# Gram products of the first three batches written to the other half's lanes, copied back by ScalarE; mask of small weights on VectorE

## The chip, the cores and the metric

One core of one Trainium2 chip. The metric is the device time of one execution in microseconds; the time before is the median of three runs, 574.6 us (570.17 to 577.01). A measurement here separates differences of about 1%.

## The reference

A linear attention with the delta rule over 4 batches, 8 heads, 768 steps and a head dimension of 48, followed by a SoLU feed-forward layer with a norm:

```python
k_n = k / (norm(k) + 1e-6)
for t in range(768):
    y[t] = q[t] @ state
    state += beta[t] * outer(k_n[t], v[t] - state.T @ k_n[t])
x = y of all heads side by side              # 3072 x 384
h = x @ w_in                                 # 384 x 1024
solu = h * softmax(h)
ln = (solu - mean) / sqrt(var + 1e-6) * g_ln
out = ln @ w_out                             # 1024 x 384
```

Inputs arrive as float64 for the weights (read as pairs of 32-bit words) and the output is float32.

## The kernel before

**Chunks and units.** The 768 steps are cut into 12 chunks (`ch`) of 64. The four batches of the input are taken in pairs (`bp`), so that a tile has 128 lanes: 64 steps of one batch of the pair (`b2` = 0) and 64 of the other (`b2` = 1). A *unit* is one chunk of one pair with its 8 heads; there are 24.

**Gram.** For each unit TensorE forms, per head and half, the products k k^T (tile `gps_`, named gram in the profile) and k q^T (tile `pps`, named qk) from the loaded tile `kq`; both are float32, and each such product is two passes in the instruction stream. Gram and qk each take one of the two buffers of the PSUM ring `fl` (`ps_f`), which the later triangular-inverse steps (sps, mps) share. VectorE multiplies qk by the causal mask into `pm`; ScalarE copies gram out.

**Batches.** The 64-step triangular systems are inverted in 7 batches `m` of chunks: batch 0 holds chunk 0 (two units), batches 1 to 5 two chunks (four units) each, batch 6 chunk 11 (two units). Within a batch the inverse of the 32 x 32 blocks (`inv_begin`, 30 `inv_step`s, `inv_end`) is an elementwise recursion with the heads on the lanes. The lanes change by a transpose. The first three batches (`SPLIT = 3`, called *near*) do this on the chip: VectorE transposes `gct` (profile name gc) into `ginv`, and the recursion is split between VectorE and POOL in blocks of 16. From batch 3 on (*far*) ScalarE copies gram to `g`, a DMA takes it through DRAM (`gd`), and POOL alone runs the recursion (tiles y and itmp). `small_level` and `block_level` (tiles sps, ssb, mps, msb, zt) then assemble the 64 x 64 inverse on TensorE.

**Where gram lies.** In a far unit gram of half `b2` is written to the lanes of the other half, `gps_[half(1 - b2)]`, while qk goes to its own half. In a near unit only three 32 x 32 blocks of gram are formed, and each is written to its own lanes, in the first 32 columns or, for the off-diagonal block, the upper 32. So one copy over 128 lanes gives `gct` (the diagonal blocks) and two copies over 32 lanes give `gxt[m][0]` (profile name gx, the off-diagonal blocks).

**Chain and feed-forward.** `chain` runs the state recursion over units (kps, ups, cps, yps on TensorE; r, st on VectorE; u on ScalarE). `moe_h` forms h from a two-part float16 split of x and of w_in in 18 matmuls, and the softmax and statistics (e, pr, ph, pl, st). `moe_out` forms the output in 24 matmuls (ops, oc).

**Weights.** `to_f32` turns the float64 words of w_in (six pieces of 512 columns) and w_out (eight of 384) into float32 on the chip: ScalarE squares the upper word (`wc`), POOL turns that into a mask that is zero for very small weights and otherwise the scale, VectorE shifts and joins the words (`wf`, for w_out `wg`), and POOL multiplies by the mask. ScalarE then rounds to float16 (`win_hi`, `wout_hi`), and POOL (for w_in) or VectorE (for w_out) forms the remainder.

**Order.** Nothing is issued in the order of the program text. A recorder collects all operations with estimated costs (`ns=...`, or a base plus a price per element for each engine) and a priority that the streams set by due times. A list scheduler over the five queues (TensorE, VectorE, ScalarE, POOL and SP for the DMAs), which also counts the free buffers of each ring, writes the final order. A change in an estimate can therefore change the order of other work. On the chip each engine runs its list in order. All recorded operations show line 266 in the profile.

The lines of the code that the change and the steps of the prediction touch:

Of the kernel before, what the change touches and what calls it, by code (L numbers as in the profile page):

```python
# [11 lines left out]
ALU = mybir.AluOpType  # L12
# [5 lines left out]
C = 64  # L18
# [288 lines left out]
def kernel(  # L307
# [26 lines left out]
    pe = Engine(rec, "PE", nc.tensor, 0, 0, 200)  # L334
    dve = Engine(rec, "DVE", nc.vector, 150, 1.04, 80)
    act = Engine(rec, "ACT", nc.scalar, 110, 0.96, 100)
    gps = Engine(rec, "POOL", nc.gpsimd, 200, 1.8, 100)
# [3 lines left out]
    def half(b2):  # L341
        return slice(C * b2, C * b2 + C)

    def dims(b2):
        return slice(C * b2, C * b2 + D)
# [4 lines left out]
    for b2 in range(2):  # L350
        nc.gpsimd.affine_select(
            out=mask[half(b2)], in_=mask[half(b2)],
# [25 lines left out]
    def to_f32(u, raw, scale, n, nm):  # L378
        if raw.dtype == F32:
            dve.tensor_scalar(out=u, in0=raw[:, :n], scalar1=scale, scalar2=None, op0=ALU.mult)  # L380
            return
        w = raw.bitcast(I32)
        lo, hi = w[:, 0 : 2 * n : 2], w[:, 1 : 2 * n : 2]
        c = p2.tile([P, 512], F32, tag="wc", name=f"wc_{nm}")[:, :n]
        act.activation(c, hi.bitcast(F32), AF.Square)
        gps.tensor_scalar(out=c, in0=c, scalar1=(1.125 * 2.0**-15) ** 2, scalar2=scale, op0=ALU.is_ge, op1=ALU.mult)
        f = u
        u = u.bitcast(I32)
        dve.tensor_scalar(out=u, in0=hi, scalar1=3, scalar2=0x3FFFFFF8, op0=ALU.logical_shift_left, op1=ALU.bitwise_and)
        dve.scalar_tensor_tensor(out=u, in0=lo, scalar=29, in1=u, op0=ALU.logical_shift_right, op1=ALU.bitwise_or)  # L390
        dve.scalar_tensor_tensor(out=u, in0=hi, scalar=-(1 << 30), in1=u, op0=ALU.bitwise_and, op1=ALU.bitwise_or)
        gps.tensor_tensor(out=f, in0=f, in1=c, op=ALU.mult)

    def load_w_in(k, q, t0, t1):
        yield t0
        f = slice(512 * q, 512 * q + 512)
        raw = p3.tile([P, 512], w_in.dtype, tag="pr", name=f"wi_{k}_{q}")
        sp.dma_start(kb=512, out=raw, in_=w_in[k, q])
        yield t1
        w = p2.tile([P, 512], F32, tag="wf", name=f"wf_{k}_{q}")  # L400
        to_f32(w, raw, SC, 512, f"i{k}{q}")
        act.copy(out=win_hi[:, k, f], in_=w)
        gps.tensor_tensor(out=win_lo[:, k, f], in0=w, in1=win_hi[:, k, f], op=ALU.subtract)
# [7 lines left out]
    def load_w_out(k, t0, t1):  # L411
        yield t0
        raw = p10.tile([P, 512], w_out.dtype, tag="kq", name=f"wo_{k}")
        sp.dma_start(kb=384, out=raw[:, :DM], in_=w_out[k])
        raws.append(rec.ops[-1])
        yield t1
        w = p2.tile([P, 512], F32, tag="wf", name=f"wg_{k}")[:, :DM]
        to_f32(w, raw, g_sb[:, k : k + 1], DM, f"o{k}")
        act.copy(out=wout_hi[:, k], in_=w)
        dve.tensor_tensor(out=wout_lo[:, k], in0=w, in1=wout_hi[:, k], op=ALU.subtract)  # L420
# [17 lines left out]
    def units(m):  # L438
        return [(ch, bp) for ch in chunks_of(m) for bp in range(2)]
# [60 lines left out]
    gct, gxt = {}, {}  # L500

    def gram(m, u, t0):
        yield t0
        ch, bp = units(m)[u]
        k = kqt[ch, bp]
        near = m < SPLIT
        if near and u == 0:
            gct[m] = p2.tile([P, 32, 32], F32, tag="y", name=f"gc_{m}")
            if len(units(m)) == 2:
                gps.memset(gct[m][:, 2 * H :], 0.0)  # L510
            gxt[m] = p2.tile([P, 4 * H, 32], F32, tag="gx", name=f"gx_{m}"), None
        g = None if near else p2.tile([P, H, C], F32, tag="g", name=f"g_{ch}_{bp}")
        pm = p10.tile([P, H, C], F32, tag="pm", name=f"pm_{ch}_{bp}")
        pt[ch, bp] = pm
        gps_ = ps_f.tile([P, H, C], F32, tag="fl", name=f"gram_{ch}_{bp}")
        pps = ps_f.tile([P, H, C], F32, tag="fl", name=f"qk_{ch}_{bp}")
        lo, up = slice(0, 32), slice(32, 64)
        for h2 in range(0, H, 2):
            with rec.atomic():
                for h, b2 in hb[2 * h2 : 2 * h2 + 4]:  # L520
                    kk = k[dims(b2), h, 0]
                    if near:
                        for r, a, b, o in ((0, lo, lo, lo), (32, up, up, lo), (32, up, lo, up)):
                            pe.matmul(
                                ns=25, out=gps_[C * b2 + r : C * b2 + r + 32, h, o], lhsT=kk[:, a], rhs=kk[:, b],
                                start=True, stop=True,
                            )
                    else:
                        pe.matmul(ns=60, out=gps_[half(1 - b2), h], lhsT=kk, rhs=kk, start=True, stop=True)
                    pe.matmul(ns=60, out=pps[half(b2), h], lhsT=kk, rhs=k[dims(b2), h, 1], start=True, stop=True)  # L530
            rec.hold(pm)
        if near:
            hs = slice(H * u, H * u + H)
            act.copy(out=gct[m][:, hs], in_=gps_[:, :, lo])
            for r in (32, 96):
                act.copy(out=gxt[m][0][r : r + 32, hs], in_=gps_[r : r + 32, :, up])
        else:
            act.copy(out=g, in_=gps_)
        dve.tensor_tensor(out=pm, in0=pps, in1=mask.unsqueeze(1).to_broadcast([P, H, C]), op=ALU.mult)
        if near:  # L540
            return
        if u == 0:
            gdt[m] = dr.tile([P, 4, H, C], F32, tag="gd", name=f"gd_{m}")
        sp.dma_start(kb=256, out=gdt[m][:, u], in_=g)
        moved[m] = rec.ops[-1]
# [346 lines left out]
    for bp in range(2):  # L892
        add(once(-14 + .1 * bp, lambda bp=bp: load_kq(0, bp), lambda bp=bp: squares(bp)))
        add(gram(0, bp, -13.5 + .01 * bp))
        add(once(-13.25, lambda bp=bp: load_kv(0, bp), lambda bp=bp: fill_v(0, bp)))
        add(tlevel(0, bp, -12.9 + 0.1 * bp, -12.85 + 0.1 * bp), -2)
# [12 lines left out]
    for m in range(1, NB):  # L909
        f = 4 * m - 2  # L910
        nu = len(units(m))
        e = f if m > 1 else f - 2.5
        for u in range(nu):
            tg = e - 9 + 0.9 * u if m > 1 else -13.34 + 0.01 * u
            ch, bp = units(m)[u]
            add(once(tg - 0.9 if m > 1 else -13.36, lambda ch=ch, bp=bp: load_kq(ch, bp)))
            add(gram(m, u, tg))
            t = e - 1.9 + 0.9 * u
            add(tlevel(m, u, t, t + 0.4))
            add(once(f + u - 1.6 if m > 1 else -12.4 + 0.1 * u, lambda ch=ch, bp=bp: load_kv(ch, bp)))  # L920
            add(once(f + u - 0.9, lambda m=m, u=u: fill_v(m, u)))
        tn = e - 5.4 if m > 1 else -12.99
        add(begin(m, tn, tn + (0.5 if m > 1 else 0.01)))
        add(inversion(m, tn + 0.6 if m > 1 else -12.97, e - 2.6 if m > 1 else -12.5))
# [81 lines left out]
```

## Time and profile before

| | |
|---|---|
| median of three runs | 574.6 us (570.17 to 577.01) |
| profiled execution | 572.56 us, of which the span of the profile is 569.9 us |
| busy share of the span | TensorE 87%, VectorE 56%, POOL 46%, ScalarE 36% |
| instructions | 21929 |
| bytes moved by DMA | 62.34 MB |

Lines of the profile give a start and a length in microseconds, the engine (PE is TensorE's matmuls, PEld its weight loads, DVE VectorE, ACT ScalarE, POOL GpSimd, SPq the queue of DMA issues), the operation as output<-inputs by the names above, the shape, and in brackets how long the engine was idle before and what ended that. Rows of groups give the count, the busy time in us, the mean of one in ns, and the idle time before. Rows of windows give for each stretch its length and, in order, the busy time of PE, PEld, DVE, ACT and POOL with counts, then the granted clock of TensorE, the DMA share and GB/s. Matmuls are pipelined, so the busy time of a group of them is the time in which at least one ran.

### The profile page before, as it was taken

How to read it: one execution, taken by the hardware profiler on the slowest of the kernel's cores; microseconds unless marked ns; L12 is line 12 of the kernel's file. 1: busy time of each engine (PE TensorE's matmuls, PEld its weight loads, DVE VectorE, ACT ScalarE, POOL GpSimd, SP SyncE). 2: the span in 40 equal slices, each digit the busy share in tenths (PEclk: the TensorE clock that was granted, in tenths of full speed). 3: DMA queues.
4: the chain of work that ended last, by engine and by line, in shares of the span. 5: the costliest groups of instructions: out<-in, count | busy, mean ns of one | idle time of the engine just before them, and what ended most of it. 6: DMA issues, size and time to landing. Idle time of an engine off the chain costs nothing.

```text
span 569.9 us, 21929 instructions
## 1 busy us (share of the span) xinstructions
PE 498.4 (87%) x9664; PEld 333.0 (58%) x9664; DVE 318.3 (56%) x795; ACT 206.8 (36%) x422; POOL 263.0 (46%) x475
## 2 busy tenths in 40 slices
PE   7989998999899577999987999969897799799983
PEld 5767777777667334656655556635564456466541
DVE  3021558838442999396615586642869546266571
ACT  1011124127341134244434444452533445345341
POOL 4051235739620564008880158840489889610100
PEclk9999999999999868989969899997799899799998
DMA  8900051202111248654469896879354594464322
GB/s 191 301 3 1 2 136 68 53 31 72 58 58 33 72 102 193 159 100 121 97 145 163 191 144 138 147 162 194 89 121 95 141 161 97 130 96 81 94 73 65
DMA packets 136606, 62.34 MB, mean 109 GB/s; under 512 B 123328, under 2 KB 126784, under 8 KB 136512
## 3 DMA queue, kind: packets, MB, share of 16 engines
q1 hardware_dynamic: 136512, 60.96, 48.8%
q8 instruction: 75, 1.23, 0.9%
q14 instruction: 19, 0.16, 0.1%
HBM read 32.10 MB, written 11.53 MB: 77 GB/s over the span
## 4 chain that ended last, share of the span: by engine, by line
PE 50%; POOL 25%; DVE 9%; issue 8%; DMA 4%; ACT 2%; SPq 1%; POOLq 0%; DVEq 0%; ACTq 0%
POOL y L266 12%; PE qk L266 11%; POOL itmp L266 11%; PE gram L266 11%; PE h L266 9%; PE ops L266 6%; PE mps L266 3%; PE ups L266 3%; PE sps L266 2%; DVE st L266 2%; DMA zt<-zd 1%; PE kps L266 1%; PE yps L266 1%; PE cps L266 1%; POOL st L266 1%
## 5 line engine op out<-in xcount | busy, mean ns | idle before, releaser
L266 PE MATMUL gram<-kq 48*32 48x32 f32 (+1 forms) x1408 | 87.4, 240 | 11.9 <-DMA kq<-kq_dram 4.0
L266 PE MATMUL h<-win_hi,xt 128*128 128x512 f16 x288 | 89.9, 432 | 6.6 <-DVE pr L266 6.3
L266 PE MATMUL qk<-kq 48*64 48x64 f32 x768 | 93.1, 274 | 0.4 <-ACT zt L266 0.2
L266 PEld LDWEIGHTS gram<-kq 48*32 48x32 f32 (+1 forms) x1408 | 63.1, 141 | 35.9 <-issue 5.3
L266 POOL TENSOR_TENSOR y<-y,itmp 128x30 f32<-128x30 f32 (+16 forms) x162 | 78.2, 483 | 12.5
L266 POOL TENSOR_TENSOR itmp<-y,ginv 128x30 f32<-128x30 f32 (+16 forms) x162 | 76.6, 473 | 12.0
L266 DVE TENSOR_REDUCE st<-h 128x1 f32<-128x1024 f32 x24 | 29.3, 1223 | 92.5 <-PE h L266 92.5
L266 PEld LDWEIGHTS <-xt 128*128 128x128 f16 x432 | 42.2, 106 | 59.1 <-issue 25.6
L266 PEld LDWEIGHTS qk<-kq 48*64 48x64 f32 x768 | 60.6, 166 | 11.3 <-ACT zt L266 0.6
L266 DVE TENSOR_TENSOR pm<-qk,mask 128x512 f32<-128x512 f32 x24 | 16.5, 687 | 72.0 <-PE qk L266 71.9
L266 PEld LDWEIGHTS <-pth 128*128 128x128 f16 x384 | 37.3, 99 | 25.1 <-issue 1.0
L266 PE MATMUL h<-win_lo,xt 128*128 128x512 f16 x144 | 47.4, 428 | 0.0
L266 ACT ACTIVATE e<-h,st 128x1024 f32<-128x1024 f32 x24 | 26.7, 1113 | 51.9 <-DVE st L266 44.6
L266 PE MATMUL ops<-wout_hi,ptl 128*128 128x384 f16 x192 | 37.3, 338 | 7.0 <-DMA ptl<-pl 7.0
L266 POOL TENSOR_TENSOR st<-st,nhalf 128x1 f32<-128x1 f32 x24 | 13.5, 562 | 64.3 <-DVE st L266 64.3
L266 ACT COPY gc<-gram 128x256 f32<-128x256 f32 x10 | 3.7, 372 | 105.1 <-PE gram L266 105.1
L266 POOL TENSOR_SCALAR_AFFINE_SELECT y<-y 128x256 f32<-128x256 f32 (+1 forms) x10 | 8.8, 892 | 70.8 <-DVE y L266 70.8
L266 POOL TENSOR_TENSOR kv<-kv,nrt 128x384 f32<-128x384 f32 x22 | 19.7, 900 | 42.7 <-DVE nrn L266 18.8
L266 DVE TENSOR_SCALAR st<-st 128x1 f32<-128x1 f32 (+1 forms) x216 | 35.5, 165 | 5.6
L266 PE MATMUL ops<-wout_lo,pth 128*128 128x384 f16 x192 | 36.4, 331 | 0.0
L266 PE MATMUL ups<-r,zt 64*64 64x48 f32 x704 | 28.1, 234 | 9.3 <-DVE r L266 6.4
L266 PE MATMUL ops<-wout_hi,pth 128*128 128x384 f16 x192 | 35.8, 328 | 0.0
(112 smaller groups left out, 909.5 us busy)
## 6 DMA issues: line engine op xcount, KB each, us to landing
kq<-kq_dram SPq DMA_DIRECT2D x48, 192.0 KB, 4.4
kv<-kv_dram SPq DMA_DIRECT2D x24, 384.0 KB, 4.0
out_dram<-oc SPq DMA_DIRECT2D x24, 192.0 KB, 2.7
gd<-g SPq DMA_DIRECT2D x14, 256.0 KB, 3.8
wi<-w_in_dram SPq DMA_DIRECT2D x6, 512.0 KB, 9.4
wo<-w_out_dram SPq DMA_DIRECT2D x8, 384.0 KB, 3.4
zd<-y SPq DMA_DIRECT2D x4, 512.0 KB, 2.6
ginv<-gd SPq DMA_DIRECT2D x12, 128.0 KB, 3.5
```

The source lines that it names most:

```text
L266: fn(*[real(a) for a in args], **{k: real(a) for k, a in kw.items()})
```

## The change

Near units now form gram as far units do: one product of 64 columns per head and half, written to the other half's lanes. ScalarE copies the four diagonal 32 x 32 blocks back across the halves (lane `r ^ 64` to lane `r`), one copy for each 32 lanes, and the two off-diagonal blocks likewise: six copies of 32 lanes instead of one of 128 and two of 32. For the scheduler a near head and half costs 60 + 60 ns instead of 75 + 60. In `to_f32` the instruction that makes the mask of small weights goes from POOL to VectorE, for all fourteen pieces.

```diff
-        gps.tensor_scalar(out=c, in0=c, scalar1=(1.125 * 2.0**-15) ** 2, scalar2=scale, op0=ALU.is_ge, op1=ALU.mult)
+        dve.tensor_scalar(out=c, in0=c, scalar1=(1.125 * 2.0**-15) ** 2, scalar2=scale, op0=ALU.is_ge, op1=ALU.mult)
...
-        lo, up = slice(0, 32), slice(32, 64)
...
-                    if near:
-                        for r, a, b, o in ((0, lo, lo, lo), (32, up, up, lo), (32, up, lo, up)):
-                            pe.matmul(
-                                ns=25, out=gps_[C * b2 + r : C * b2 + r + 32, h, o], lhsT=kk[:, a], rhs=kk[:, b],
-                                start=True, stop=True,
-                            )
-                    else:
-                        pe.matmul(ns=60, out=gps_[half(1 - b2), h], lhsT=kk, rhs=kk, start=True, stop=True)
+                    pe.matmul(ns=60, out=gps_[half(1 - b2), h], lhsT=kk, rhs=kk, start=True, stop=True)
                     pe.matmul(ns=60, out=pps[half(b2), h], lhsT=kk, rhs=k[dims(b2), h, 1], start=True, stop=True)
...
-            act.copy(out=gct[m][:, hs], in_=gps_[:, :, lo])
+            for r, c in ((0, 0), (32, 32), (64, 0), (96, 32)):
+                act.copy(out=gct[m][r : r + 32, hs], in_=gps_[r ^ 64 : (r ^ 64) + 32, :, c : c + 32])
             for r in (32, 96):
-                act.copy(out=gxt[m][0][r : r + 32, hs], in_=gps_[r : r + 32, :, up])
+                act.copy(out=gxt[m][0][r : r + 32, hs], in_=gps_[r ^ 64 : (r ^ 64) + 32, :, 0:32])
```

## The prediction

> **What bounds the kernel now.** I read the page's chain of work first, then the list of waits.
>
> ```profile
> PE 50%; POOL 25%; DVE 9%; issue 8%; DMA 4%; ACT 2%; SPq 1%; POOLq 0%; DVEq 0%; ACTq 0%
> POOL y L266 12%; PE qk L266 11%; POOL itmp L266 11%; PE gram L266 11%; PE h L266 9%; PE ops L266 6%; PE mps L266 3%; PE ups L266 3%; PE sps L266 2%; DVE st L266 2%; DMA zt<-zd 1%; PE kps L266 1%; PE yps L266 1%; PE cps L266 1%; POOL st L266 1%
> ...
> ACT gc L266 <- PE gram L266: 105.1, 10, 11.8
> DVE pm L266 <- PE qk L266: 71.9, 11, 12.2
> ```
>
> TensorE holds half of the chain, and gram and qk alone are 22% of it, some 125 of 569.9 us. The waits say which: ten times ScalarE stood about 10.5 us before a gc copy. gc exists only in the first three batches, so these are the ten "near" units (two of batch 0, four each of batches 1 and 2), which I number 1 to 10 in order of time. The far units' copies (tile g) are not there. Next, one near unit in the timeline:
>
> ```profile
> 16.99 0.43 PE L266 MATMUL gram<-kq 48*32 48x32 f32 x6 [0.81 <-ACT gx L266]
> 17.35 0.47 PE L266 MATMUL qk<-kq 48*64 48x64 f32 x2
> 17.75 0.42 PE L266 MATMUL gram<-kq 48*32 48x32 f32 x6
> ...
> 28.65 0.47 PE L266 MATMUL qk<-kq 48*64 48x64 f32 x2
> 28.75 0.37 ACT L266 COPY gc<-gram 128x256 f32<-128x256 f32 x1 [11.82 <-PE gram L266]
> 29.15 0.74 ACT L266 COPY gx<-gram 32x256 f32<-32x256 f32 x2
> 29.16 0.69 DVE L266 TENSOR_TENSOR pm<-qk,mask 128x512 f32<-128x512 f32 x1 [12.18 <-PE qk L266]
> 29.76 2.00 DVE L266 STREAM_TRANSPOSE ginv<-gc 128x1024 f32<-128x1024 f32 x1
> ```
>
> Each head and half costs 0.76 us (16.99 to 17.75) for eight passes: six of 32 columns, two of 64. Sixteen of these make 12.1 us (16.99 to 29.1). The groups do not overlap: qk starts when gram's last pass is nearly done, and the next gram 0.40 us later. Now the far form, which writes gram to the other half, and the two state products beside it, also 64 by 64:
>
> ```profile
> L266 PE MATMUL gram<-kq 48*64 48x64 f32 x32 | 1.4, 223 | 0.0
> L266 PE MATMUL qk<-kq 48*64 48x64 f32 x32 | 1.4, 224 | 0.0
> ...
> L266 PE MATMUL cps<-u,kv 64*64 64x48 f32 x32 | 2.0, 305 | 0.0
> L266 PE MATMUL yps<-u,pm 64*64 64x48 f32 x32 | 2.0, 305 | 0.0
> ```
>
> The first two rows are one far unit at 212.6 us: 64 passes in 1.4 us, interleaved. The last two lie in the first 110 us: 64 interleaved passes in 2.0 us. So the same count of passes that the changed near unit would have takes 1.4 to 2.0 us when all have one shape and go to four quadrants, against 12.1 us now.
>
> **The change: the products.** A near unit goes from 16 x (6 + 2) = 128 passes of two shapes to 64 of one. Which of 1.4 and 2.0 us? The clock decides:
>
> ```profile
> 184.00:186.00 2.00, 2.00 (x26) 0.97 (x21) 1.98 (x2) 0.00 (x0) 0.00 (x0) 1.00 0.24 18
> 188.00:190.00 2.00, 1.90 (x9) 0.69 (x7) 1.73 (x10) 0.00 (x0) 0.00 (x0) 1.00 0.28 62
> ...
> 185.31 1.49 PE L266 MATMUL h<-win_lo,xt 128*128 128x512 f16 x3
> 186.59 2.02 PE L266 MATMUL h<-win_hi,xt 128*128 128x512 f16 x6
> 188.44 0.81 PE L266 MATMUL h<-win_lo,xt 128*128 128x512 f16 x3
> 189.09 0.81 PE L266 MATMUL h<-win_hi,xt 128*128 128x512 f16 x3
> ```
>
> The granted clock (the third number from the end) reads 1.00 in both stretches, yet three h passes take 1.28 us from 185.31 and 0.65 us from 188.44. The near stage really runs at the slow cadence, whatever the column says, so I take 2.1 us per unit: 10.0 us less of TensorE, 100 us over ten units. This is not yet the gain; the rest of this part finds what was behind those units.
>
> The Trainium skill speaks against the change here: its page "TensorE: Matmul & The Clock Gate", Part 1, says that a TensorE idle for a window of about 3.4 us falls to half clock, and the change leaves it idle more. By that rule the stage's other matmuls would slow down; the h rows show them slow already, so I charge nothing in the main sum and keep the rule's remainder as a rival.
>
> **The copies.** ScalarE goes from three copies per unit (0.37 us each, 0.40 from start to start) to six, 2.3 us instead of 1.1. No row shows a copy that crosses lanes; the gx copy (32 lanes, 0.37) is the nearest and the one I take. Below it, nothing excludes a few per cent; above, twice as much would be 2.3 us more per unit. The copies hold the gram buffer (two buffers, one for gram, one for qk), so the next unit waits for them: +1.2 us wherever ScalarE ends last.
>
> **First stage, up to the second transpose.** Rows at which the new queues stand:
>
> ```profile
> 13.70 0.18 DVE L266 TENSOR_SCALAR nn<-nb 128x32 f32<-128x32 f32 x1
> ...
> 45.21 0.22 POOL L266 TENSOR_TENSOR y<-y,itmp 128x14 f32<-128x14 f32 x1
> ...
> 55.58 0.17 DVE L266 TENSOR_TENSOR itmp<-y,ginv 128x14 f32<-128x14 f32 x1
> ...
> 61.94 0.18 DVE L266 TENSOR_TENSOR y<-y,itmp 128x14 f32<-128x14 f32 x1
> 67.88 0.69 DVE L266 TENSOR_TENSOR pm<-qk,mask 128x512 f32<-128x512 f32 x1 [5.75 <-PE qk L266]
> ...
> 72.43 1.91 DVE L266 STREAM_TRANSPOSE gy<-ginv 128x1024 f32<-128x1024 f32 x1
> ...
> 81.42 2.10 DVE L266 STREAM_TRANSPOSE ginv<-gc 128x1024 f32<-128x1024 f32 x1
> ```
>
> I keep each engine's order. VectorE makes the norms until 13.9, then the first mask pm until 14.6; only then is a buffer free for unit 2: products to 16.8, copies to 19.1. The transpose ginv starts at 19.1 (29.76 before), and POOL's half of the inversion, which ended 15.7 us after the transpose began (45.43), ends at 34.8. Units 3 and 4 follow at 2.1 + 2.3 us each: products done at 21.2 and 25.7, pm of unit 4 at 26.4. VectorE's half of the inversion takes 6.5 us alone (55.58 to 62.12); beside POOL's I give it until 35.0. From pm of unit 5 to the end of gy is 6.5 us without a gap (67.88 to 74.34), plus two new masks of 0.4: 42.3. With unit 6's pm (its products are long done) the transpose of batch 1 starts at 42.9, not 81.42: **-38 us**, not 60, since the norms, ScalarE and both inversions come forward as the bound. The loads of the six units do not bind:
>
> ```profile
> 4.04 5.05 SPq L266 DMA_DIRECT2D kq<-kq_dram  x8
> ...
> kq<-kq_dram SPq DMA_DIRECT2D x48, 192.0 KB, 4.4
> ```
>
> SP has issued the last of their twelve at 9.1 us, at a median of 4.4 us to landing; even twice that is ahead of the 34.8 at which unit 6 wants its own.
>
> **Later stage.** Up to 108 us VectorE is the chain (norms and inversion of batch 1 beside unit 7), so unit 7 brings **0**. Then:
>
> ```profile
> 122.24 0.62 ACT L266 CAST win_hi<-wf 128x512 f16<-128x512 f32 x1
> ...
> 124.13 0.43 DVE L266 TENSOR_SCALAR wf<-wi 128x512 int32<-128x512 int32 x1 [9.37 <-POOL win_lo L266]
> ...
> 161.61 0.69 DVE L266 TENSOR_TENSOR pm<-qk,mask 128x512 f32<-128x512 f32 x1 [11.41 <-PE qk L266]
> ...
> 182.15 0.69 DVE L266 TENSOR_TENSOR pm<-qk,mask 128x512 f32<-128x512 f32 x1 [10.26 <-PE qk L266]
> ```
>
> Unit 8: win_hi is queued on ScalarE behind its copies, POOL behind win_hi, VectorE behind POOL, idle for 9.37. Products 10.0 shorter, copies 1.2 longer, little else waiting: **-8.4**. Unit 9: VectorE waits for qk only: **-10**. Unit 10: the copies show in the transpose behind it, partly under pl: **-9.5**.
>
> **The mask of small weights.** Fourteen instructions move from POOL to VectorE. Between 120 and 152 us:
>
> ```profile
> L266 POOL TENSOR_SCALAR wc_o<-wc_o,g_sb 128x384 f32<-128x384 f32 x5 | 8.2, 1643 | 0.5
> ...
> L266 POOL TENSOR_SCALAR wc_i<-wc_i 128x512 f32<-128x512 f32 x2 | 4.1, 2070 | 0.2
> ...
> L266 DVE TENSOR_SCALAR wg<-wo 128x384 int32<-128x384 int32 x4 | 3.3, 836 | 0.1
> ...
> L266 DVE TENSOR_SCALAR wf<-wi x6: 379/424/1469, 68.5 to 129.6; 128x512 int32<-128x512 int32 x6
> ...
> 81.40:182.20 100.80, 94.79 (x2039) 73.44 (x2039) 58.84 (x126) 37.15 (x87) 52.26 (x69) 1.00 0.18 53
> ```
>
> POOL loses 12.3 us there; VectorE pays 0.42 each where it is undisturbed, up to 0.84 beside POOL, 7 x 0.42 = 2.9 here. POOL is nearly full between 124 and 151, so its relief shows, but VectorE is next: **-2.5**, with bounds of -6 and +3. VectorE's 58.8 busy us, plus some 4.6 for eleven masks, fit into 100.8 - 30.4 = 70.4 us, though at 90%; this is why I take no more. The steady part after about 190 us keeps its order and its POOL and TensorE chain: 0.
>
> **Sum.** 38 + 8.4 + 10 + 9.5 + 2.5 = 68.4. The profiled execution took 572.56 us (569.9 span, 2.7 around it), 0.4% under the median of 574.6 and inside its three runs. 572.6 - 68.4 = **504 us**. Its own range is 488 to 522: copies twice as long on eight units (+18), masks +-4, VectorE's inversion up to 2 early, a dozen us from the queues' order.
>
> **Rivals.** The order of all instructions is written by a planner from estimated costs, and the diff alters three of them (near unit 2.16 to 1.92 us, three more copies, masks on VectorE). *The reshuffle gives gain back:* if only the first stage's 38 us stay and the later units' holes fill with VectorE work, 535. For: VectorE at 90%. Against: the holes are TensorE's. Chance 0.10. *More is gained:* if the planner puts the norms and pm's so that no queue stands in between, the whole 100 go, 472. For: POOL and ScalarE are busy 52.3 and 37.2 of the 100.8 us of the later stage. Chance 0.12. *The clock:* TensorE falls into slow cadence after the stage too, two units' h (36 passes x 0.21 us), +8: 512. Chance 0.07. *Slower:* the passes of 64 columns are slow in themselves. A qk pass takes 0.20 us here (0.40 for two); if 64 of them cost that in a row, a unit takes 12.8 + copies 2.3 instead of 12.1 + 1.1; ten times 1.9, less 2.5, gives 589. It decides once a pass costs more than about 0.17 us. Against it stand the far unit and cps, 64 passes in 1.4 and 2.0. Chance 0.03. The skill's page "TensorEngine Tiling (Array Packing)", Gotcha 1, would have it so (different row tiles cannot write one PSUM bank at once, and both halves write one gram tile); the far unit, which does just that, shows no such stall.
>
> **How the numbers follow.** Forecast 0.68, rivals as given. About 1% (6 us) is what a measurement of this kernel can tell. Between 478 and 535 lie the forecast, the clock case and half of each of the two order cases; what is left out is most of a full gain and the slower case. Faster by over 1%: 0.95; within 1%: 0.02; slower: 0.03.
>
> **What would show it.** Near units of 1.4 to 2.3 us and no ScalarE wait of 10 us for gram; the 32-lane copies at 0.37; the second transpose of batch 1 near 43 us, that of batch 2 near 116; masks on VectorE at 0.4; the time from there to the end about as before (386 us). Units still near 12 us, copies over 0.7, or a longer stretch behind the third transpose would make it wrong.

## The result, and the profile after

The changed kernel takes 0.9015 of the time before (95% interval 0.893 to 0.910): 515.3, 517.5 and 519.9 us against a median of 574.7, a gain of about 57 us. The forecast was 504 us (range 478 to 535), a gain of 68. A fourth execution, the one that was profiled, was a slow run of 869.0 us and is not counted, so the profile shown here is of a further execution of the changed kernel, with a span of 512.3 us.

The chain of work and the top of the list of waits, as they were shown of before:

```profile
PE 28%; POOL 26%; DVE 24%; issue 11%; SPq 4%; DMA 4%; ACT 3%; POOLq 0%; DVEq 0%; ACTq 0%
...
DVE st L266 <- PE h L266: 69.4, 17, 7.5
POOL y L266 <- DVE y L266: 67.3, 4, 26.7
```

TensorE falls from half of the chain to 28%; the 105 us in which ScalarE waited for gram are gone. One near unit (the third), grouped over 18.7 to 21 us, and its copies in the timeline:

```profile
L266 PE MATMUL qk<-kq 48*64 48x64 f32 x32 | 2.0, 314 | 1.1 <-ACT gx L266 1.1
L266 PE MATMUL gram<-kq 48*64 48x64 f32 x30 | 2.0, 314 | 0.0
...
20.83 1.49 ACT L266 COPY gc<-gram 32x256 f32<-32x256 f32 x4 [2.07 <-PE qk L266]
22.33 0.74 ACT L266 COPY gx<-gram 32x256 f32<-32x256 f32 x2
```

The unit's products take 2.0 us in place of 12.1, the six copies 2.2 us. Now the three gram transposes on VectorE (batches 0, 1, 2):

```profile
18.10 2.08 DVE L266 STREAM_TRANSPOSE ginv<-gc 128x1024 f32<-128x1024 f32 x1 [0.86 <-ACT gc L266]
...
40.91 2.03 DVE L266 STREAM_TRANSPOSE ginv<-gc 128x1024 f32<-128x1024 f32 x1
...
114.81 2.10 DVE L266 STREAM_TRANSPOSE ginv<-gc 128x1024 f32<-128x1024 f32 x1
```

The forecast had 19.1, 42.9 and 116. So up to 115 us the kernel does what was said, and the 11 us that are missing lie behind. The same cuts in windows, before and after: up to the transpose of batch 1, to that of batch 2, to POOL's start on batch 5 (its affine select), to the end.

```profile
0.00:81.40 81.40, 72.82 (x768) 54.80 (x768) 23.70 (x66) 10.75 (x25) 22.83 (x56) 1.00 0.42 111
81.40:184.00 102.60, 96.59 (x2091) 74.86 (x2095) 60.64 (x128) 37.82 (x88) 52.26 (x69) 1.00 0.18 52
184.00:406.50 222.50, 188.32 (x4442) 119.59 (x4437) 141.36 (x371) 89.33 (x180) 103.50 (x196) 0.91 0.67 140
406.50:569.90 163.40, 140.68 (x2374) 83.77 (x2374) 92.60 (x234) 68.94 (x131) 84.44 (x155) 0.93 0.50 104
```

```profile
0.00:40.90 40.90, 14.71 (x384) 12.45 (x384) 25.18 (x65) 17.56 (x43) 18.49 (x55) 1.00 0.81 206
40.90:114.80 73.90, 54.34 (x1851) 43.65 (x1852) 62.11 (x131) 39.04 (x94) 35.01 (x57) 1.00 0.26 70
114.80:349.80 235.00, 195.66 (x4417) 125.82 (x4415) 143.59 (x374) 90.44 (x181) 101.42 (x195) 0.85 0.64 135
349.80:512.30 162.50, 139.00 (x2379) 83.47 (x2374) 94.29 (x242) 70.89 (x135) 84.77 (x155) 0.94 0.53 104
```

The first stage gives 40.5 us, the second 28.7, the last 0.9; the third, which the change does not touch but for a few late weights, is **12.5 us longer**. POOL and VectorE have about as much to do in it as before (101.4 against 103.5 us, 143.6 against 141.4); they wait more. TensorE is busy 7.3 us longer (195.7 against 188.3) for about as many matmuls, at a lower granted clock (0.85 against 0.91). In the second stage VectorE is now busy 62.1 of 73.9 us (84%), more than any other engine, as expected.

### The profile page after: what moved, and what is told of

It reads as the page before. It is cut to its first block, busy times and chain, and to the rows that moved or that the text cites. A ratio compares the mean times of both kernels' runs of the same rounds, so it can differ in the third digit from the quotient of the medians.

```text
span 866.9 us, 20677 instructions
## 1 busy us (share of the span) xinstructions
PE 814.3 (94%) x9024; PEld 443.0 (51%) x9024; DVE 326.8 (38%) x809; ACT 218.9 (25%) x452; POOL 232.7 (27%) x461
## 3 DMA queue, kind: packets, MB, share of 16 engines
q8 instruction: 70, 1.15, 0.6%
## 4 chain that ended last, share of the span: by engine, by line
PE 88%; DVE 7%; DMA 1%; issue 1%; ACT 1%; SPq 0%; POOL 0%; DVEq 0%; ACTq 0%; POOLq 0%
PE ops L266 30%; PE h L266 29%; PE ups L266 6%; PE cps L266 5%; PE kps L266 4%; PE mps L266 4%; PE gram L266 3%; PE yps L266 3%; PE sps L266 2%; PE qk L266 2%; DVE y L266 1%; DVE itmp L266 1%; DVE wf L266 1%; PE cs L266 1%; DMA kn<-kn_dram 1%
## 5 line engine op out<-in xcount | busy, mean ns | idle before, releaser
L266 PE MATMUL h<-win_hi,xt 128*128 128x512 f16 x288 | 183.7, 804 | 7.3 <-DVE pr L266 4.7
L266 PEld LDWEIGHTS <-xt 128*128 128x128 f16 x432 | 65.1, 159 | 143.6 <-issue 141.8
L266 PE MATMUL ops<-wout_hi,ptl 128*128 128x384 f16 x192 | 87.6, 666 | 4.7 <-DMA ptl<-pl 4.7
L266 PE MATMUL ops<-wout_lo,pth 128*128 128x384 f16 x192 | 91.6, 685 | 0.0
L266 PE MATMUL ops<-wout_hi,pth 128*128 128x384 f16 x192 | 91.5, 688 | 0.0
L266 PE MATMUL gram<-kq 48*64 48x64 f32 x768 | 65.1, 365 | 22.6 <-DVE pm L266 13.4
L266 PEld LDWEIGHTS gram<-kq 48*64 48x64 f32 x768 | 59.0, 272 | 33.0 <-DVE pm L266 14.0
L266 DVE SCALAR_TENSOR_TENSOR oc<-csum,st,ops 128x384 f32<-128x384 f32 x24 | 14.7, 614 | 139.4 <-PE ops L266 139.4
L266 PEld LDWEIGHTS cps<-u,kv 64*64 64x64 f32 x704 | 51.2, 280 | 17.2 <-issue 11.0
L266 PEld LDWEIGHTS ups<-r,zt 64*64 64x64 f32 x704 | 51.5, 280 | 16.1 <-issue 13.9
L266 PE MATMUL yps<-u,pm 64*64 64x48 f32 x768 | 59.1, 331 | 0.0
L266 PEld LDWEIGHTS kps<-st,kq 48*64 48x64 f32 x704 | 51.9, 283 | 10.7 <-issue 10.5
```

The source lines that it names most:

```text
L266: fn(*[real(a) for a in args], **{k: real(a) for k, a in kw.items()})
```

## The experiments

Two questions were open: where the 12.5 us of the third stage went, and what made a near unit take 12.1 us. The scheduler's freedom can be taken away: it orders by the costs that it is told, so a kernel can do one work in the order written for another. Below, "old order" is the list of before on every engine, "new order" that of the changed kernel, each apart from the instructions that are replaced. In the traces of the runs said to be in one order, VectorE, ScalarE, POOL and SP go through the same instructions one after the other, but for those replaced.

**The changed kernel again.**

> The changed kernel once more, for a profile whose steady part runs at full clock. Theory A (the gain is the near products; what is missing against the forecast's 504 us was lost to the planner's new order): near units of 1.4 to 2.3 us, the transpose of batch 2's gram near 116 us, and a stretch behind it of about 400 us, 14 longer than the 386 before. Theory B (the first stage itself gained less, because VectorE with its masks and the longer copies bound it): the transpose of batch 2 near 130 us and the stretch behind it 386 us. Time 515 to 520 us under both.

Measured: 515.4 us, ratio 0.9001 (0.8952 to 0.9051); the cuts are those above. The second transpose and the third are where theory A put them, and the stretch behind is 397.5 us, not 386. Theory B falls.

**Only the products, old order.** The mask stays on POOL, and the scheduler is told the old costs:

```diff
-                    pe.matmul(ns=60, out=gps_[half(1 - b2), h], ...)
+                    pe.matmul(ns=75 if near else 60, out=gps_[half(1 - b2), h], ...)
-                act.copy(out=gct[m][r : r + 32, hs], ...)
+                act.copy(ns=110 + 0.96 * 256 if r == 0 else 0, out=gct[m][r : r + 32, hs], ...)
```

> Only the near products and their copies are changed, the mask stays on POOL, and the scheduler is told the costs of before, so that every engine's list is that of before but for the replaced instructions. Theory A: 572.6 - 66 = 506 us, the transpose of batch 2 near 118 us, the stretch behind it 386 us. Theory B: 518 us or more, with the transpose at 130 us.

Measured: 505.0 us, ratio 0.8797 (0.8751 to 0.8843). The transposes are at 41.6 and 113.4 us; POOL starts on batch 5 at 338.9, 225.5 behind the transpose. So the total comes out within 2 us of the forecast's working (506) once the old order, its assumption, is enforced. In part that is luck: the first two stages gained more than was summed up for them without the mask (39.8 and 30.8 us against 38 and 27.9), and the third took 3.0 us more.

**The whole change, old order.** The mask runs on VectorE, but is planned as if on POOL:

```diff
+    pod = Engine(rec, "POOL", nc.vector, 200, 1.8, 100)
...
-        gps.tensor_scalar(out=c, in0=c, ...)
+        pod.tensor_scalar(out=c, in0=c, ...)
```

> The whole change in the order of before: as the run before, and the mask's fourteen instructions on VectorE at the place in the issue order that POOL had for them. Theory A: 504 us, the forecast. Theory B: as the changed kernel, 518 us. If the mask on VectorE in itself costs time, this is slower than the products alone in the old order.

Measured: 505.4 us, ratio 0.8794 (0.8747 to 0.8841). So the changed kernel's own instructions take 505 us in the old order and 515 in their own: this loss of 10 us is the order's. The cuts of this run:

```profile
0.00:42.20 42.20, 14.70 (x384) 12.45 (x384) 26.80 (x68) 18.67 (x45) 19.57 (x55) 1.00 0.75 193
42.20:115.70 73.50, 52.66 (x1849) 43.68 (x1850) 62.77 (x138) 39.84 (x96) 34.49 (x59) 0.69 0.29 80
115.70:343.20 227.50, 189.61 (x4421) 121.09 (x4419) 140.96 (x372) 90.12 (x182) 99.11 (x194) 0.89 0.69 138
343.20:506.60 163.40, 141.56 (x2374) 84.73 (x2373) 92.63 (x234) 69.03 (x131) 84.38 (x155) 0.92 0.53 104
```

Against the changed kernel it is the third stage that differs most: 227.5 in place of 235.0 us. (The profiled execution is the slowest of the four here, 508.4 us, and the fastest of the changed kernel's, 514.5, so the stages show less of a difference than the medians.) One place where the time goes can be seen on SP. First the changed kernel, then this one, around the loads that bring batch 4's gram back from DRAM (ginv<-gd):

```profile
254.86 0.38 SPq L266 DMA_DIRECT2D gd<-g  x1
...
261.72 1.23 SPq L266 DMA_TRANSPOSE pth<-ph  x1
263.07 1.23 SPq L266 DMA_TRANSPOSE ptl<-pl  x1
264.35 1.29 SPq L266 DMA_TRANSPOSE xt<-x  x1
266.09 0.36 SPq L266 DMA_DIRECT2D out_dram<-oc  x1
266.52 3.12 SPq L266 DMA_DIRECT2D ginv<-gd  x4
...
279.30 1.27 POOL L266 TENSOR_SCALAR_AFFINE_SELECT y<-y 128x1024 f32<-128x1024 f32 x1 [17.90 <-DVE y L266]
```

```profile
247.02 0.38 SPq L266 DMA_DIRECT2D gd<-g  x1
...
251.18 3.36 SPq L266 DMA_DIRECT2D ginv<-gd  x4
...
260.20 1.26 SPq L266 DMA_TRANSPOSE pth<-ph  x1
...
269.41 1.26 POOL L266 TENSOR_SCALAR_AFFINE_SELECT y<-y 128x1024 f32<-128x1024 f32 x1 [9.45 <-DVE y L266]
```

In the new order the loads stand behind one unit's three transposes and an output, 11.7 us after the last gd in place of 4.2, and that gd itself is 8.7 us later after the transpose of batch 2 (140.1 against 131.3). POOL, which has the largest part of the chain, stands idle 17.9 in place of 9.45 us, and starts on batch 4 9.9 us later. This wait goes with the list in every run: 17.5 to 17.9 us where the list was written with the mask planned on VectorE, 6.4 to 9.5 in all others. On VectorE the norms of batch 4 come behind the maximum of one more unit's h as well (nine in place of eight), so the loads alone would probably not bring it back. The new order also leaves five of the fourteen masks behind the third transpose, in place of two, and TensorE's longer busy time goes with it (195.3 to 196.4 us in the third stage at a granted clock of 0.85 to 0.87 with such a list, 185.9 to 190.3 at 0.88 to 0.91 without). Which of these weighs how much was not tried one by one.

**Only the products, with the order that the scheduler then writes.** The mask stays on POOL, the costs are the new ones.

> Only the products and copies, mask on POOL, with the scheduler's costs as they then are, so a third order. Theory A: between 500 and 525 us, and not the same as the products in the old order, since the order alone differs from it. Theory B: within 1% of the products in the old order.

Measured: **499.2 us**, ratio 0.8699 (0.8657 to 0.8740), the fastest of all, and just under the range that was expected. Its third stage takes 220.9 us. A third order, then, with its own worth: 1% better than the old one, 3% better than the changed kernel's.

**The new order with the mask on POOL.** `dve` in the mask's line is replaced by an engine that is planned as VectorE and runs on POOL.

> The changed kernel in its own order, but the fourteen mask instructions run on POOL, at the place in the issue order that VectorE has for them. Theory A (the order costs the missing 10 us, the mask's engine is worth nothing): 515 us, as the changed kernel. Rival (the mask on VectorE costs time in this order): near 505 us. Rival (the mask on POOL costs here, as POOL is the chain): 525 us.

Measured: 521.2 us, ratio 0.9122 (0.9070 to 0.9174), 1.3% slower than the changed kernel: a result between theory A and its second rival. The third stage is 237.7 us, the new order's length again, but the second is 78.7 in place of 73.9. In the new order, then, the mask on VectorE is worth some 6 us, which is little more than a measurement can separate; in the old order it was worth nothing.

**The work of before in the new order.**

```diff
-                                ns=25, out=gps_[C * b2 + r : ...
+                                ns=20, out=gps_[C * b2 + r : ...
-            act.copy(out=gct[m][:, hs], ...)
+            act.copy(ns=4 * (110 + 0.96 * 256), out=gct[m][:, hs], ...)
...
+    dvp = Engine(rec, "DVE", nc.gpsimd, 150, 1.04, 80)
...
-        gps.tensor_scalar(out=c, in0=c, ...)
+        dvp.tensor_scalar(out=c, in0=c, ...)
```

> The work of before (three 32-column products, three copies, mask on POOL) in the order of the changed kernel: the scheduler is told the changed kernel's costs. Theory A (the new order in itself costs about 10 us behind the first stage): 574 + 10 = 584 us. Rival (the new order costs only with the short near units): 574 us.

Measured: 590.5 us, ratio 1.0343 (1.0269 to 1.0418). Not one operation differs from before, and it is 3.4% slower, 6 us more than was expected. The third transpose and POOL's start on batch 5:

```profile
189.03 2.04 DVE L266 STREAM_TRANSPOSE ginv<-gc 128x1024 f32<-128x1024 f32 x1
...
426.22 1.26 POOL L266 TENSOR_SCALAR_AFFINE_SELECT y<-y 128x1024 f32<-128x1024 f32 x1 [25.80 <-DVE y L266]
```

107.4 us from the second transpose (at 81.6) to the third in place of 102.6, and 237.2 us to batch 5 in place of 222.5. This third stage is about as long as in the changed kernel (235.0) and in the run before (237.7).

**Only the mask, the scheduler told so; and only the mask, old order.** The first takes the one line of the diff that moves the mask, the second the `pod` engine above.

> Only the mask goes to VectorE, with the scheduler told so; products and copies are those of before. Its order of issue is close to the changed kernel's. Theory A2 (the move of the mask is what makes the scheduler write the worse order): slower than before by 10 to 20 us, 584 to 592 us. Rival (the worse order comes from the costs of products and copies): 572 us or less, as the sum of the forecast had it (-2.5).

> Only the mask's fourteen instructions on VectorE, issued at the place that POOL had for them in the order of before; all else is before. Theory A2: no difference, 570 to 575 us, since in that order the mask's engine is worth nothing. Forecast's term: -2.5 us, 569.5.

Measured: 586.2 us, ratio 1.0232 (1.0193 to 1.0270), and 572.2 us, ratio 0.9998 (0.9968 to 1.0028). The same fourteen instructions on the same engine: nothing in the old order, 14 us when the scheduler may order anew. The list of the first run is not quite the new order, but in both cases in which the scheduler was told of the mask's move (here, and the changed kernel against the products alone) its list was worse by 14 to 16 us: it is the one line about the mask that does it.

**The whole change in the order of the products alone.**

> The whole change in the order that the scheduler writes for the products alone (499 us with the mask on POOL), with the mask on VectorE at POOL's places. Theory A2: 499 us, within 1%. If the mask on VectorE frees POOL where it counts in this order, as in the changed kernel's own (6 us), 493.

Measured: 504.8 us, ratio 0.8810 (0.8771 to 0.8849). Not the 499 that was expected: with the mask on VectorE this order is 1.3% slower, the intervals apart. Across the three orders that move is worth 0, 6 us gained and 6 us lost. By the cuts it loses 2.0 us in the first stage and 1.6 in the third; why was not settled.

**What a near unit spent: own lanes.** The 64-column product goes to its own half's lanes, as qk does; every list is the changed kernel's.

```diff
-                    pe.matmul(ns=60, out=gps_[half(1 - b2), h], ...)
+                    pe.matmul(ns=60, out=gps_[half(b2 if near else 1 - b2), h], ...)
-                act.copy(out=gct[m][r : r + 32, hs], in_=gps_[r ^ 64 : (r ^ 64) + 32, :, c : c + 32])
+                act.copy(out=gct[m][r : r + 32, hs], in_=gps_[r : r + 32, :, c : c + 32])
```

> The changed kernel with one difference: the 64-column gram product of a near unit is written to its own half's lanes, where qk goes too, and the six copies cross no lanes. Every list is the same as the changed kernel's. Theory A1 (a near unit took 12.1 us because its passes alternate between two shapes): the unit stays near 2 us and the time at 515 us, within 1% of the changed kernel. Rival A2 (it took so long because gram and qk of a half share one quadrant of the array and must go one after the other): the unit goes back toward 10 us and the time toward 565 us. The copies: 0.36 us each with or without a crossing.

Measured: 521.3 us, ratio 0.9099 (0.9033 to 0.9165). The unit, grouped over 20.5 to 24.2 us, and its copies:

```profile
L266 PE MATMUL qk<-kq 48*64 48x64 f32 x32 | 3.7, 313 | 0.9 <-ACT gx L266 0.9
L266 PE MATMUL gram<-kq 48*64 48x64 f32 x30 | 3.5, 313 | 0.0
...
24.00 1.49 ACT L266 COPY gc<-gram 32x256 f32<-32x256 f32 x4 [3.57 <-PE gram L266]
```

3.7 us in place of 2.0: sharing the quadrant (the same lanes in and the same lanes out) costs 1.7 us a unit. The whole is some 6 us slower than the changed kernel (515.4), but the intervals overlap. It is not what took 12. The four copies take 1.49 us with and without a crossing of lanes.

**Grouped by shape.** Before, but in each atomic group the twelve 32-column products first, then the four qk products:

```diff
                 for h, b2 in hb[2 * h2 : 2 * h2 + 4]:
                     ...                          # near: the three gram products
+                        continue
...
+                if near:
+                    for h, b2 in hb[2 * h2 : 2 * h2 + 4]:
+                        pe.matmul(ns=60, out=pps[half(b2), h], lhsT=k[dims(b2), h, 0], rhs=k[dims(b2), h, 1], ...)
```

> The kernel before, with one difference: in each of a near unit's four atomic groups the twelve 32-column gram products come first and the four qk products after them, so that the shape alternates 4 times a unit in place of 16; blocks, lanes, copies, mask and every list are those of before. Theory A1 (shapes): a switch pair costs (0.755 - 8 passes at 0.03) = 0.5 us, so a unit takes 128 x 0.03 + 4 x 0.5 = 6 us in place of 12.1, and the time falls by some 45 us to about 528. Rival A2 (shared quadrant): nothing changes, 574 us.

Measured: 514.7 us, ratio 0.9011 (0.8956 to 0.9065). Reordering the matmuls within near units alone, with the same blocks, lanes, copies and mask, brings as much as the whole change did in its own order, and 13 us more than the 528 expected; in the same old order the whole change reaches 505. Two of a unit's four groups:

```profile
19.38 0.67 PE L266 MATMUL gram<-kq 48*32 48x32 f32 x24 [0.62 <-ACT gx L266]
19.99 0.69 PE L266 MATMUL qk<-kq 48*64 48x64 f32 x8
20.61 0.67 PE L266 MATMUL gram<-kq 48*32 48x32 f32 x24
21.21 0.69 PE L266 MATMUL qk<-kq 48*64 48x64 f32 x8
```

24 passes of 32 columns take 0.61 us from start to start, where 6 took 0.36 before (16.99 to 17.35 in the prediction's rows); 8 of 64 columns take 0.62, where 2 took 0.40. A straight line through the two points of each gives an estimate: about 0.014 us a pass and 0.28 a switch for the one, 0.037 and 0.33 for the other. A unit before switched 32 times, which would be 9.7 of its 12.1 us. The change of half between heads is not what costs: the grouped stretches alternate between the halves too. Theory A1 holds, with its size a little under (4.9 us a unit against the 6 expected). A 32-column product is narrower both in its weights and in what streams past them; which of the two makes the switch was not told apart.

## Why the prediction was right, and where not

The stages of the runs that bear on it, in us (cuts as above, each read from the same rows of that run; the second column is what a near unit's products take):

| run | near unit | order | to batch 1 | to batch 2 | to batch 5 | to the end |
|---|---|---|---|---|---|---|
| before | 12.1 | old | 81.4 | 102.6 | 222.5 | 163.4 |
| forecast | 2.1 | old | 42.9 | 73 | 222.5 | 163.4 |
| products, old order | 2.0 | old | 41.6 | 71.8 | 225.5 | 163.2 |
| whole change, old order | 2.0 | old | 42.2 | 73.5 | 227.5 | 163.4 |
| changed kernel | 2.0 | new | 40.9 | 73.9 | 235.0 | 162.5 |
| new order, mask on POOL | 2.0 | new | 40.9 | 78.7 | 237.7 | 162.2 |
| work of before, new order | 12.1 | new | 81.6 | 107.4 | 237.2 | 162.4 |
| products only | 2.0 | third | 41.5 | 72.0 | 220.9 | 163.5 |
| whole change, third order | 2.0 | third | 43.5 | 72.2 | 222.5 | 163.6 |
| mask only, old order | 12.1 | old | 81.2 | 103.9 | 222.0 | 163.0 |
| mask only | 12.1 | its own | 81.8 | 107.4 | 229.6 | 164.3 |

- **Near units** (100 us less of TensorE): right. 2.0 us at the slow cadence, as taken from cps, not from the far unit.
- **First stage** (-38): right, measured -40.5. The queues named were the ones: the first mask pm comes right behind the norms (13.75 us), the second unit's products wait for it, and the transpose of batch 0 waits for ScalarE (0.86 us, the row above).
- **Copies** (0.37 us each, six): right. The tile's answer for the changed kernel gives

```profile
L266 ACT COPY gc<-gram x40: 360/364/368, 8.6 to 114.1; 32x256 f32<-32x256 f32 x40
```

- **Second stage** (-8.4, 0, -10, -9.5, and -2.5 for the mask, together -30.4): right as a sum; -30.8 for the products alone in the old order, -29.1 with the mask. So the **mask's -2.5 was wrong**, and the products brought that much more; that the sum came out is luck. (Ten of the masks lay in this stretch before, not eleven, which changes the sum of VectorE's work by 0.4 us.) VectorE pays for a mask what was taken in the median, though the longest took 1.15 us, above the 0.84 that was allowed:

```profile
L266 DVE TENSOR_SCALAR wc_o<-wc_o,g_sb x8: 408/418/1150, 91.3 to 148.5; 128x384 f32<-128x384 f32 x8
```

  What failed is that POOL's relief would show: in the old order the mask alone is 0.9998, and with the short units the second stage is 73.5 us with it and 71.8 without. VectorE, busy 62.8 of the 73.5 us, is probably the next bound there; no run isolates it.
- **"The steady part keeps its order: 0"**: this is the step that failed, +12.5 us, and by the prediction's own sign: 386 us were to lie behind the third transpose, and 397.5 do. The sum had it at nothing; only the forecast's own range (488 to 522) left a dozen us for the queues' order, and that is what the measured time needed. The rival of the reshuffle was there, but with its price in the wrong place (the second stage, 535 us) and with a chance of 0.10. The order costs the changed kernel 10 us, for the most part in the third stage; the remaining 3 to 5 us of the 12.5 are there in the old order too and stay open. The cause of the order is the mask's line: it changes what the scheduler is told of POOL and VectorE, and the list gets 14 us slower even with the rest of before (586.2 us; there 5 us of it lie in the second stage and 7 in the third).
- **The rival of more gained** (472) did not come: the norms stayed in between (pm of unit 1 at 13.75 us). The products alone with a third order reach 499.
- **The clock** rival cannot be told apart. Its 8 us would have stood in the third stage. In the old order that stage is still 3.0 us (products) and 5.0 us (whole change) longer than before, at a granted clock of 0.89 against 0.91 in the second case; this may be the rival at half its price, and stays open. It does not by itself make the 12.5, since the work of before, with its long near units, has the same long stage and low clock in the new order (237.2 us at 0.86): there the clock goes with the order. Whether the lower clock adds to the order's 10 us, or only comes of the waits, no run shows. That the Trainium skill's page "TensorE: Matmul & The Clock Gate" (Part 1) makes an idle TensorE slow agrees with the unit at 2.0 us in the first stage, where TensorE is busy 14.7 of 40.9 us and far units take 1.4 later. But the page's rule is not the whole of it here: before the change TensorE was busy 96.6 of 102.6 us in the second stage, and the prediction's h rows right behind it still run at the slow cadence.
- **The slower rival** fell: passes of 64 columns cost 0.03 to 0.04 us, and two row tiles writing one bank did not hold each other up; the halves share the gram tile in the 2.0 us unit too.

Against the Trainium skill's page "TensorEngine Tiling (Array Packing)", Key Properties, which says that a change of tiling mode drains the array, the grouped run agrees and gives it a size here: about 0.3 us a switch, by the estimate above.

## What to carry to other kernels

Small matmuls of different shapes that alternate are worth sorting by shape before anything else: that alone gave 10% here without a change of layout or of copies. Where a list scheduler writes the order from estimated costs, a change in any estimate is a change of the whole program; run the new work in the old order and the old work in the new before a gain or loss is put down to the work. And a long stage in which one engine is "busy" through such switches hides idle engines whose queues are then the next bound; walk each queue in order, as the stage after the change ends with them.

## What the runs showed of the hardware that was not expected

A switch between products of 32 and of 64 columns (48 by 32 and 48 by 64 weights) costs about 0.3 us at the slow cadence, twenty times a small pass (0.014 us), by the estimate from the grouped run. The granted clock in the windows cannot be taken for the clock in use early in a trace: the second stage reads 1.00 in the changed kernel and 0.69 in the whole change in old order, with 54.3 and 52.7 us of TensorE for the same work, and the prediction's h rows run at two cadences under a reading of 1.00. Copies out of PSUM that cross from one half of the lanes to the other take the same time as those that do not (four in 1.49 us in both).
